# Fourteen products of the identity on TensorE while the first two chunks load

## The chip, the cores and the metric

One core of a Trainium2 chip. The metric is device microseconds (us) of one execution; lower is better. Executions of the same kernel spread by 2 to 3 us. The experiments ran in three batches, each on another chip, each with nine runs of the kernel before beside it; differences are taken within a batch unless the text says otherwise. The "granted clock" of a run is the mean share of full speed that the profile's records give TensorE.

## The reference

Retention over 64 (batch, head) sequences of 576 positions and 64 columns, followed by a maxout FFN:

```python
scores = (1 / sqrt(64)) * q @ k.T                    # per batch and head
ret = (scores * D) @ v                               # D[i, j] = gamma_h ** (i - j), 0 above the diagonal
x = ret, rearranged to (4608, 512)
h = maximum(maximum(x @ w1, x @ w2), x @ w3)         # (4608, 768), weights in float64
out = h @ w_out                                      # (4608, 512)
```

## The kernel before

The sequence is taken in 36 chunks of 128 positions. For each chunk K is scaled on GpSimd (POOL), K and Q are transposed on TensorE (PE), then come the scores, the state and the values. A group of four chunks feeds one pass of the FFN. The float64 weights arrive as integers, and VectorE (DVE), ScalarE (ACT) and POOL turn them into float32, piece by piece. The parts that matter here:

```python
def transposes(g):
    for n, src in (("k", kds[g]), ("q", raws.pop(("q", g)))):
        pt = ps_r.tile([P, NP, C], FP32, tag="r", name=n + "t")
        for p in range(NP):                              # NP = 4
            nc.tensor.transpose(pt[:, p, :], pair(src, p), ident[:C, :C])
        # ... copied to SBUF, K by DVE, Q by ACT

def scores(g):                                           # cut
    # 8 products s = K.T @ Q of 64 rows; DVE masks them: st
    for p in range(NP):
        nc.tensor.matmul(kv[:, p, :], lhsT=pair(kd, p)[r:], rhs=pair(raws["v", g], p)[r:], start=True, stop=True)
    # ... the state is made of kv on DVE and POOL

def down(t, h, m):                                       # cut
    for fb in range(NF):                                 # NF = 6: waits for each piece of w_out
        nc.tensor.matmul(ps[:], lhsT=h[:, fb, m * P:(m + 1) * P], rhs=w_sb["out", fb][:],
                         start=(fb == 0), stop=(fb == NF - 1))

# the beginning
load(0); load(1); load(2); load_weights(1); load(3); load_weights(2)
decay_keys(0); decay_keys(1)                             # POOL: kd
transposes(0)
transposes(1)
decay_keys(2)
scores(0)
transposes(2)
values(0)
decay_keys(3)
scores(1)
convert(4)                                               # first piece of the weights
transposes(3)
# ... cut
```

## Time and profile before

| | before |
|---|---|
| median of the first 3 runs | 888.28 us (887.31 to 889.44) |
| span of the profiled run, granted clock | 887.5 us, 0.996 |
| first transposes, first products at full speed | 5.21 us, 15.0 us |
| first weight conversion (expo) starts | 19.99 us |
| first `up` product starts | 35.21 us |
| first `down` product with the last piece of w_out | 121.10 us |

In the timeline a row has start, length, engine, line, operation, output<-inputs, shape and count, then the idle time before it and what ended it. In the chain of waits a row has start, length, and what held the end of the program at that time. In the table of windows below each row is a stretch of time: busy time and instructions of PE, its weight loads, DVE, ACT and POOL, then the granted clock, the DMA share and GB/s. Of the kernel before:

```profile
120.00:121.00 1.00, 0.00 (x0) 0.00 (x0) 0.00 (x0) 0.00 (x0) 1.00 (x1) 0.88 0.00 0
121.00:122.00 1.00, 0.90 (x1) 0.50 (x2) 0.00 (x0) 0.00 (x0) 1.00 (x2) 0.50 0.00 0
...
127.00:128.00 1.00, 1.00 (x3) 0.51 (x3) 0.69 (x1) 0.00 (x0) 0.00 (x0) 0.70 0.06 16
```

The clock column is at 0.50 from within the first row to within the last. In the first 15 us the same column shows 1.00.

### The profile page before, as it was taken

The page shows a single profiled execution, that of the slowest core. Times are in us where ns is not written, and L with a number is a line of the kernel's source. Part 1 is how long each engine was busy: PE and PEld are TensorE (multiplying, and loading weights), DVE is VectorE, ACT ScalarE, POOL GpSimd, SP SyncE. Part 2 cuts the span into 40 slices and gives each one's busy share as a digit, 9 for nine tenths or more (in the row PEclk, how much of TensorE's full clock was granted, in tenths as well). Part 3 has the DMA queues.
Part 4 walks back from the last instruction along what each step waited for, and adds up shares of the span by engine and source line. Part 5 has one row for each costly group of instructions (what it writes and reads, how often), then busy time and mean ns, then how long its engine had stood idle before and what let it go on. Part 6 is the DMA issues. An engine that isn't in the chain of part 4 may idle for free.

```text
span 887.5 us, 11310 instructions
## 1 busy us (share of the span) xinstructions
PE 870.8 (98%) x4544; PEld 639.5 (72%) x4544; DVE 371.4 (42%) x681; ACT 185.8 (21%) x391; POOL 141.4 (16%) x128
## 2 busy tenths in 40 slices
PE   6999989999999999999999999999999999999998
PEld 5645546887588858885788668875888578866883
DVE  3899944553244423443244324432433334422330
ACT  2455521111111102111111111111111111111211
POOL 3444424221110111001210011101111111001000
PEclk9999989999999999999999999999999999999999
DMA  9545614200150006000600033001600050000001
GB/s 235 154 138 173 179 49 121 57 1 12 57 123 1 1 36 154 1 1 24 147 21 1 13 96 83 1 1 49 142 1 1 24 130 1 0 25 24 1 1 47
DMA packets 128547, 51.58 MB, mean 58 GB/s; under 512 B 113648, under 2 KB 122864, under 8 KB 128496
## 3 DMA queue, kind: packets, MB, share of 16 engines
q1 hardware_dynamic: 128064, 50.34, 21.5%
q8 instruction: 36, 0.59, 0.3%
q10 hardware_dynamic: 432, 0.53, 0.2%
q14 instruction: 15, 0.12, 0.0%
HBM read 41.42 MB, written 9.44 MB: 57 GB/s over the span
## 4 chain that ended last, share of the span: by engine, by line
PE 87%; DVE 5%; ACT 3%; issue 2%; POOL 1%; DMA 1%; SPq 0%; DVEq 0%; POOLq 0%; ACTq 0%
PE x L292 28%; PE down L338 21%; PE z L292 14%; PE y L292 7%; PE s L155 4%; PE o L185 3%; PE kv L166 3%; PE o L190 3%; PE kt L141 2%; PE qt L141 2%; ACT expo L244 1%; ACT expo L248 1%; DVE expo L241 1%; DVE expo L252 1%; DVE h L352 1%
## 5 line engine op out<-in xcount | busy, mean ns | idle before, releaser
L338 PE MATMUL down<-wout,h 128*128 128x512 f32 x432 | 191.7, 597 | 3.8 <-POOL wout L255 3.8
L338 PEld LDWEIGHTS down<-wout,h 128*128 128x128 f32 x432 | 80.5, 191 | 96.5 <-issue 90.7
L292 PE MATMUL x<-S,T 128*128 128x256 f32 x576 | 147.8, 379 | 0.0
L292 PEld LDWEIGHTS x<-S,T 128*128 128x128 f32 x576 | 109.2, 190 | 15.1
L172 POOL TENSOR_TENSOR state<-state,gs 128x512 f32<-128x512 f32 x24 | 31.5, 1311 | 343.5 <-DVE state L171 296.5
L158 DVE TENSOR_TENSOR st<-s,causal 128x512 f32<-128x512 f32 x72 | 46.4, 686 | 76.5 <-PE s L155 76.5
L292 PE MATMUL x<-xT,w 128*128 128x256 f32 x288 | 74.9, 382 | 0.0
L292 PE MATMUL x<-S,w 128*128 128x256 f32 x288 | 74.3, 380 | 0.0
L292 PE MATMUL z<-xT,T 128*128 128x256 f32 x288 | 73.9, 379 | 0.0
L292 PE MATMUL z<-S,w 128*128 128x256 f32 x288 | 73.9, 379 | 0.0
L292 PE MATMUL y<-xT,w 128*128 128x256 f32 x288 | 73.9, 379 | 0.0
L297 ACT COPY p<-x 128x256 f32<-128x256 f32 x72 | 26.8, 372 | 182.8 <-PE x L292 182.8
L320 DVE TENSOR_TENSOR tmp<-x,p 128x256 f32<-128x256 f32 x48 | 20.4, 425 | 104.4 <-PE x L292 104.4
L347 PE MATMUL up<-xT,w 128*128 128x512 f32 x144 | 63.4, 593 | 0.0
L341 ACT COPY osb<-down 128x512 f32<-128x512 f32 x36 | 21.1, 586 | 202.1 <-PE down L338 202.1
L292 PEld LDWEIGHTS z<-S,w 128*128 128x128 f32 x288 | 54.7, 190 | 7.4
L292 PEld LDWEIGHTS y<-xT,w 128*128 128x128 f32 x288 | 54.7, 190 | 7.4
L292 PEld LDWEIGHTS z<-xT,T 128*128 128x128 f32 x288 | 54.1, 189 | 8.1
L292 PEld LDWEIGHTS x<-S,w 128*128 128x128 f32 x288 | 49.4, 189 | 13.2 <-issue 1.1
L192 DVE TENSOR_TENSOR xT<-o,gq 128x512 f32<-128x512 f32 x36 | 24.8, 690 | 72.8 <-PE o L190 66.8
L292 PEld LDWEIGHTS x<-xT,w 128*128 128x128 f32 x288 | 49.8, 191 | 5.5 <-issue 0.8
L130 POOL TENSOR_TENSOR kd<-kraw,gk 128x512 f32<-128x512 f32 x36 | 38.3, 1068 | 85.5 <-DMA kraw<-in_k_dram 74.9
(61 smaller groups left out, 913.9 us busy)
## 6 DMA issues: line engine op xcount, KB each, us to landing
bits<-in_moe_w_dram SPq DMA_DIRECT2D x18, 512.0 KB, 3.6
out_dram<-osb SPq DMA_DIRECT2D x36, 256.0 KB, 2.0
kraw<-in_k_dram SPq DMA_DIRECT2D x32, 256.0 KB, 4.0
qraw<-in_q_dram SPq DMA_DIRECT2D x32, 256.0 KB, 4.3
vraw<-in_v_dram SPq DMA_DIRECT2D x32, 256.0 KB, 4.3
bits<-in_moe_w_out_dram SPq DMA_DIRECT2D x6, 512.0 KB, 3.4
kraw<-in_k_dram SPq DMA_DIRECT2D x8, 128.0 KB, 3.6
qraw<-in_q_dram SPq DMA_DIRECT2D x8, 128.0 KB, 3.2
```

The source lines that it names most:

```text
L130: nc.gpsimd.tensor_tensor(t[:], raws.pop(("k", g))[:], gk[:].unsqueeze(2).to_broadcast([C, H, D]), op=ALU.mult)
L141: nc.tensor.transpose(pt[:, p, :], pair(src, p), ident[:C, :C])
L155: nc.tensor.matmul(s[j][:, p, :], lhsT=kT[r, p, :], rhs=qT[r, p, :], start=True, stop=True)
L158: nc.vector.tensor_tensor(st[:, j], s[j][:], masks[start_of(g)][:].unsqueeze(1).to_broadcast([C, NP, C]), op=ALU.mult)
L166: nc.tensor.matmul(kv[:, p, :], lhsT=pair(kd, p)[r:], rhs=pair(raws["v", g], p)[r:], start=True, stop=True)
L172: nc.gpsimd.tensor_tensor(t[:], t[:], gs[:], op=ALU.mult)
L185: nc.tensor.matmul(o[D * j:D * (j + 1), p, :], lhsT=vr[:, 2 * p + j, :], rhs=st[:, j, p, :], start=(p == 0), stop=(old == 0 and p == NP - ...
L190: nc.tensor.matmul(o[:, p, :old], lhsT=sd[:, p, :], rhs=qT[:, p, :old], start=False, stop=(p == NP - 1), skip_group_check=True)
L292: nc.tensor.matmul(out[:], lhsT=w[:, d * P:(d + 1) * P], rhs=xS[t][n][:, d, :], start=first and d == 0, stop=d == 1, skip_group_check=True)
L297: nc.scalar.copy(c[:], src[:])
L338: nc.tensor.matmul(ps[:], lhsT=h[:, fb, m * P:(m + 1) * P], rhs=w_sb["out", fb][:], start=(fb == 0), stop=(fb == NF - 1))
L347: nc.tensor.matmul(ps[:], lhsT=w_sb[i, fb][:, dc * P:(dc + 1) * P], rhs=xT[t][:, dc, :], start=(dc == 0), stop=(dc == NDC - 1))
```

## The change

The intent is that the array finds its full clock before the first real work needs it. TensorE multiplies the identity with itself while it would wait for the first loads; nobody reads the results.

```diff
+    def warm(n):
+        ps = ps_y.tile([P, P], FP32, tag="y", name="warm")
+        for _ in range(n):
+            nc.tensor.matmul(ps[:], lhsT=ident[:], rhs=ident[:], start=True, stop=True)
...
+    warm(9)
     load(0)
...
     transposes(0)
+    warm(5)
     transposes(1)
```

## The prediction

> **What bounds the kernel now.** I read the page first, slices and chain, then the chain of waits in order of time, the TensorE timeline of the first 24 us, the granted clock around 121 us and the landing of the first loads. From the page:
>
> ```profile
> span 887.5 us, 11310 instructions
> PE   6999989999999999999999999999999999999998
> PE 87%; DVE 5%; ACT 3%; issue 2%; POOL 1%; DMA 1%; SPq 0%; DVEq 0%; POOLq 0%; ACTq 0%
> ```
>
> The reader is to see that TensorE (PE) carries 87% of the path. It is idle only in the first slice (22.2 us each) and near 120 us. Whatever 14 more matmuls can bring lies in the first slice. The chain of waits, from its beginning, says which idle time counts (start us, length us, what):
>
> ```profile
> 3.05 5.06 DMA kraw<-in_k_dram
> 8.18 1.05 POOL kd L130
> 9.27 1.11 PE kt L141 x4
> 10.38 0.85 PE qt L141 x4
> 11.24 2.01 PE s L155 x16
> 13.25 1.92 PE kv L166 x8
> ...
> 16.05 1.02 PE o L185 x16
> 17.07 1.14 PE s L155 x16
> ...
> 20.08 0.35 DVE expo L241
> ...
> 119.78 1.27 POOL wout L255
> ...
> 121.10 2.07 PE down L338 x2
> ```
>
> So the load of the second K chunk and its scaling on POOL hold the path until 9.23 us; then TensorE holds it to 18.2; then the conversion of the float64 weights on DVE and ACT (rows expo, mant, frac) to 121.05; from there TensorE to the end. Conversion of one piece waits for the one before, so whatever moves its first step moves everything behind it. The timeline of TensorE shows what its 9 us are made of (start, length, operation):
>
> ```profile
> 5.21 1.12 PE L141 MATMUL kt<-ident,kd 128*128 128x128 f32 x4 [5.21 <-POOL kd L130]
> ...
> 11.17 2.08 PE L155 MATMUL s<-qT,kT 64*128 64x128 f32 x16
> 13.18 1.99 PE L166 MATMUL kv<-vraw,kd 128*128 128x128 f32 x8
> 15.01 0.60 PE L141 MATMUL kt<-ident,kd 128*128 128x128 f32 x4
> ...
> 17.00 1.16 PE L155 MATMUL s<-qT,kT 64*128 64x128 f32 x16
> 18.09 1.16 PE L166 MATMUL kv<-vraw,kd 128*128 128x128 f32 x8
> ```
>
> The same 16 score products take 2.08 us at 11.17 and 1.16 at 17.00; the same 8 kv products 1.99 and 1.16. The array ran at half speed until about 15.0 us, although the clock column of the page says 9 to 10 tenths there: no record covers this first stretch, only durations do. Half speed on the path is what the change aims at.
>
> **What the Trainium skill says.** (1) "TensorE: Matmul & The Clock Gate", Part 1: the array starts at half clock and goes to full after about one busy window of 3.4 us; the window is free-running. The trace agrees with halves, and with the period: in windows of one microsecond the granted clock is 0.88 in 120 to 121 and 0.70 in 127 to 128 with 0.50 between, so it fell at 120.76 and rose at 127.60, 6.84 us or two windows of 3.42. Stepped back 33 windows of the page's 3.413 us, 127.60 becomes 14.96, just where the durations halve. (2) The same page, "Why this matters for your kernels": keep TensorE busy 4 us or more, and leave no gap over about 3 us. (3) The same page, Part 4, says that transposes don't count as busy in the same way. The trace can't settle that, but the transposes do run faster once warm (1.12 us to 0.60 for four). No page says how busy a window must be.
>
> **The change part by part.** It removes and moves nothing. It adds 14 products of a 128x128 identity with itself, and two allocations from the two-buffer PSUM tag "y"; two keep the rotation where it was, nobody reads them, and the tag is not used again before the first `up` at 35 us. They need only the identity.
>
> Cost of one: the kv row is the same form (128 rows, 128 columns, fp32): in the chain 1.92 to 2.00 us for 8 cold, so 0.25 us; 1.09 for 8 warm, 0.14.
>
> Nine of them: the identity is finished on POOL at 1.38 (its last instruction starts at 1.09 and takes 0.29); plus about 0.1 of hand-over, start at 1.5. 9 x 0.25 = 2.25, end at 3.75. kd(0) lets the first transposes start at 5.21. So they delay nothing, and leave a gap of 1.46 us.
>
> Five of them: the first transposes end about 7.45; 5 x 0.25 = 1.25, end at 8.7. The next transposes start at 9.27. No delay, a gap of 0.57 us.
>
> So the direct cost on the path is nil and the benefit depends on when the clock rises. **If it is up by 9.27**, the path goes (warm durations from the later rows): kt and qt 0.88 to 10.15, s 1.09 to 11.24, kv 1.09 to 12.33. There it meets the third chunk: kd(2) is done at 12.72 (POOL from 11.68 for 1.04, released by a load), so transposes go 12.78 to 13.66, o 1.02 to 14.7, and s(1) starts at 14.7 in place of 17.0. Of a possible 2.85 us (half of 9.27 to 14.96), 0.45 is lost to that wait, leaving about 2.3. The masks and the state of chunk 1 then let the first expo start about 17.8 instead of 19.99; its weights landed at 16.5 (issued 10.62, 5.9 to landing), no obstacle. The fourth K chunk lands at 17.45 and kd(3) ends at 18.63 whatever TensorE does, so its transposes come only 0.3 earlier (18.98 to 18.7). With DVE taking its list in order I get s(2) ending and its mask ending at 24.1 against 25.6, the state of chunk 3 at 24.8 against 26.2, and the first `up` at 33.5 against 35.1: **about 1.6 us** that survive, and TensorE and the conversion both carry them on to 121 and so to the end.
>
> **How likely is it to be up?** On this trace's grid of windows (1.31, 4.72, 8.13, 11.55, 14.96):
> before, 8.13 to 11.55 was busy 9.27 to 11.55, 67%, and didn't raise it; 11.55 to 14.96, all busy, did. Near 121, the window 120.76 to 124.18 was busy from 121.10, at most 90%, and didn't raise it; the next, all busy, did. So a window must be nearly full. With the change: 1.31 to 4.72 is busy 2.25 of 3.41, 66%; 4.72 to 8.13 busy 5.21 to 8.13, 86%; 8.13 to 11.55 busy all but 0.57, 83%. By those precedents **none is enough**, and the clock would rise at 14.96 as before. At other phases the run 5.21 to 8.7, 3.5 us long, can hold a window, if transposes count.
>
> **Rivals.**
> A: the clock is up before 9.27, as intended. For it: the run of 3.5 us, an unknown threshold, and that nobody picks 9 and 5 without a reason. Against it: the two gaps. Gain 1.6 us against this profiled run; but its rise at 14.96 was late. If a window must start after 8.8 us, the rise before lies anywhere from 12.2 to 15.6; as 1.25 of the cold loss is absorbed, the mean gain over phases is about 1.1. Chance 0.4.
> B: the gaps undo it, and the time stays. For it: the precedents above and the page's Part 4. Chance 0.5.
> C: faster early TensorE is hidden anyway, since loads set the pace (POOL waited 12.0 us for K loads in the first 45 us). In part counted above: the loads of the third and fourth chunk eat 1.25 of 2.85. If the later conversion waits for a load at the earlier time too, A is worth 0.5. Chance 0.1.
> D: the added products are slower than kv, 0.43 each (four passes of 128 columns at the half clock would give that), and fill both gaps: nine end at 5.4, five at 9.6. That costs 0.2 to 0.3 and makes A sure. Against it: the kv rows. Included in A's chance.
>
> **Range and chances.** 0.4 x 1.1 + 0.1 x 0.5 = 0.5 us: 888.28 - 0.5 = 887.8; I put 887.7. The times of before spread over 887.31 to 889.44, and the phase of the clock's windows, at the start and again at 121 us, is reason enough for it. A full gain on a good median is 886; no gain on a poor one 889.2. Range 886.0 to 889.2. 2% is 17.8 us, over six times the whole cold loss of 2.85 us: same 0.97, faster 0.02, slower 0.01.
>
> **What would show it right or wrong.** In the timeline of the changed kernel: nine products from about 1.5, at a spacing of 0.25 us, and the end near 3.75 (D if near 5.3); five from 7.45 to 8.7; kt of chunk 0 still at 5.21 and of chunk 1 at 9.27. Then the score products at 11 us: 2.08 us long means B, 1.16 means A. With A: s(1) near 14.7, first expo near 17.8, first `up` near 33.5, first `down` pair after the conversion near 119.5 instead of 121.1. With C the first three move and the last does not. The prediction is wrong if transposes start late because of the added products, if `up` waits for the PSUM tag, or if the idle time near 118 us, falling on other windows, costs more or less than the cold stretch of 121.10 to 127.60 does now.

## The result, and the profile after

The changed kernel took 887.35 us (median of 6 runs, 886.27 to 888.40); the kernel before, with three more runs beside them, 888.56 (6 runs). The ratio is 0.9987, 95% interval 0.9974 to 1.0000: the same within 2%, as predicted, and close to the predicted 887.7. The interval reaches 1.0000, so this comparison alone doesn't show a gain. All outputs are right. A ratio is the mean time of one kernel's runs over the mean of the other's of the same rounds, so not quite the ratio of the medians.

From the page of the changed kernel, then its TensorE timeline:

```profile
span 884.6 us, 11367 instructions
```

```profile
1.43 4.21 PE L108 MATMUL warm<-ident 128*128 128x128 f32 x18 [1.43 <-POOL ident masks.py:199]
5.43 1.06 PE L147 MATMUL kt<-ident,kd 128*128 128x128 f32 x4
6.43 0.88 PE L147 MATMUL qt<-ident,qraw 128*128 128x128 f32 x4
7.15 1.28 PE L108 MATMUL warm<-ident 128*128 128x128 f32 x10
9.35 0.66 PE L147 MATMUL kt<-ident,kd 128*128 128x128 f32 x4 [0.91 <-POOL kd L136]
...
10.37 1.16 PE L161 MATMUL s<-qT,kT 64*128 64x128 f32 x16
...
15.02 1.16 PE L161 MATMUL s<-qT,kT 64*128 64x128 f32 x16
...
18.54 0.66 PE L147 MATMUL kt<-ident,kd 128*128 128x128 f32 x4 [1.27 <-POOL kd L136]
```

The reader should see three things. **First, x18 and x10:** each of the 9 and 5 products is two records, so nine fill the time from 1.43 to the first transposes (5.43 less 1.43 is 4.00, 0.44 us a product) where I had 2.25. There is no gap before 8.4 us. **Second,** the scores of chunk 0 take 1.16 us at 10.37 where they took 2.08 at 11.17: the clock was up. It rose at about 6.95, to judge by the fall and rise near 121 (119.58 and 123.00, and 34 windows of 3.413 us back from 123.00); the shorter row qt at 6.43 agrees, and the clock record in the trace file, which begins at the first rise, says 6.94. **Third,** the last row: TensorE now waits 1.27 us for kd(3). The chain of waits of the changed kernel says who brought it:

```profile
11.83 5.45 DMA kraw<-in_k_dram
...
17.44 1.05 POOL kd L136
18.49 0.04 issue
18.54 0.66 PE kt L147 x4
```

The load of the fourth K chunk has taken over the path that TensorE held from 9.27 to 18.2. What that leaves, in the two profiled runs:

| | before | after | earlier by |
|---|---|---|---|
| scores of chunk 1 start | 17.00 | 15.02 | 1.98 |
| first conversion (expo) starts | 19.99 | 18.01 | 1.98 |
| transposes of chunk 4 start | 34.28 | 32.80 | 1.48 |
| first `up` starts | 35.21 | 33.73 | 1.48 |
| `down` with the last piece starts | 121.10 | 119.59 | 1.51 |
| values (o) after the first `down` products start | 132.53 | 129.58 | 2.95 |
| span | 887.5 | 884.6 | 2.9 |

So 1.98 us was gained at the scores, 0.5 given back to the load, and 1.5 carried through the conversion to 121 us. The other 1.4 us appear after 121, where the change touched nothing. Here are the windows of the changed kernel there:

```profile
119.00:120.00 1.00, 0.41 (x1) 0.41 (x2) 0.00 (x0) 0.00 (x0) 1.00 (x2) 0.79 0.00 0
...
122.00:123.00 1.00, 1.00 (x12) 1.00 (x12) 0.00 (x0) 0.29 (x1) 0.00 (x0) 0.50 0.08 16
123.00:124.00 1.00, 1.00 (x14) 0.88 (x10) 0.56 (x1) 0.00 (x0) 0.00 (x0) 1.00 0.65 248
```

The half-clock stretch lasts 3.42 us here, one window, and 6.84, two windows, in the profile of before. Such a run has a granted clock of 0.998, the other kind 0.996. The profiled pair therefore flatters the change, and the experiments have to separate the two.

### The profile page after: what moved, and what is told of

Same layout as the page of the kernel before. It is cut to its first block, busy times and chain, and to the rows that moved or that the text cites. A ratio compares the mean times of both kernels' runs of the same rounds, so it can differ in the third digit from the quotient of the medians.

```text
span 884.6 us, 11367 instructions
## 1 busy us (share of the span) xinstructions
PE 871.5 (99%) x4572; PEld 640.8 (72%) x4572; DVE 371.4 (42%) x681; ACT 185.8 (21%) x391; POOL 141.5 (16%) x128
## 4 chain that ended last, share of the span: by engine, by line
PE 87%; DVE 5%; ACT 3%; issue 2%; SPq 1%; POOL 1%; DMA 1%; POOLq 0%; DVEq 0%; ACTq 0%
PE x L298 28%; PE down L344 21%; PE z L298 14%; PE y L298 7%; PE s L161 4%; PE o L191 3%; PE o L196 3%; PE kv L172 3%; PE kt L147 2%; PE qt L147 1%; ACT expo L250 1%; ACT expo L254 1%; DVE expo L247 1%; SPq L131 1%; DVE expo L258 1%
```

## The experiments

**Theory 1**: the products fill the windows, the clock rises before 9.3 us, and the path gains until the loads stop it. **Rival, luck**: the time moves only because the windows near 121 us fall otherwise. **Rival, place or number**: any product there helps, or only one of the two batches does. In each table "granted" lists the clocks of the 5 runs.

### The changed kernel twice more

> The changed kernel once more, on the chip of the other runs of this call. Theory 1 (the early clock): TensorE is busy from 1.43 to 7.4 us without a gap, a full window of 3.41 us always fits, the clock rises between 4.9 and 8.3 us, s of chunk 0 takes 1.16 us; 0.5 to 1.6 us less than before, and the same difference between runs of the same granted clock (0.996 with 0.996, 0.998 with 0.998). Rival (luck of the windows near 121 us): runs of the same granted clock differ by under 0.3 us from before.

> The changed kernel again, on the chip of these runs, for comparison. Theory 1: 0.7 to 2.0 us less than before; granted clock 0.996 to 0.998 in each run, never 0.994 or less (no fall in the first 20 us). Rival (luck): no difference from before when runs of 0.996 are compared with runs of 0.996.

| | mean, us | median, us | before, median | ratio (95%) | granted |
|---|---|---|---|---|---|
| after_again | 886.95 | 886.78 | 889.04 | 0.9978 (0.9965 to 0.9992) | 0.996 x2, 0.998 x3 |
| after_third | 886.40 | 885.71 | 888.65 | 0.9973 (0.9960 to 0.9985) | 0.996 x2, 0.998 x3 |

Both are faster than before. At equal granted clock, over all runs that have a clock on record (16 of the changed kernel, 32 of the kernel before, whose first six have none), chips mixed: at 0.996, 887.77 (8 runs) against 888.86 (26 runs); at 0.998, 886.07 (8) against 888.12 (6). Theory 1 asked for a difference within a class and finds 1.1 and 2.05; luck alone asked for under 0.3. The classes are not quite like with like, for the same clock can cost differently: of its 6.83 us at half clock near 121, the profiled run of after_third has a first window that is 52% busy, that of before one that is 90% busy. So the filled kernels below have to settle it. All in all, 886.92 against 888.72: 1.8 us, 0.2%. The gains of the means in the two batches, 1.9 and 2.3 us, are larger than expected (0.5 to 1.6, and 0.7 to 2.0).

The detail expected of after_again failed: its transposes of Q waited 0.60 us for a load, which left the window from 4.03 to 7.44 only 82% busy, and the clock was not up by 8.3 us but at about 10.85 (its fall at 120.08 less 32 windows). The second batch was cold, 2.34 us long, and the transposes of chunk 1 partly so (0.96 for kt, then 0.60 for qt). The scores still ran in 1.16 us.

### One batch alone

```diff
# first_only             # second_only            # small
     warm(9)             -    warm(9)             -    warm(9)
...                      ...                      +    warm(3)
-    warm(5)                  warm(5)             ...
                                                  -    warm(5)
                                                  +    warm(2)
```

> The nine products alone. Theory 1: the busy run 1.43 to about 7.4 us still holds a full window, and the gap of about 1.8 us to the transposes of chunk 1 empties none, so the clock rises by 8.3 us, s of chunk 0 takes 1.16 us and the gain is that of the changed kernel within 0.3 us. If the five products are needed to keep the clock, s of chunk 0 takes 2.08 us again in the profile and the gain is under 0.4 us.

> The five products alone. At the cold 0.44 us each they last from 7.4 to 9.6, delay the transposes of chunk 1 by about 0.3 us, and TensorE is busy from 5.21 on without a gap. Theory 1: the clock rises between 8.6 and 12.0 us, so part of s or kv of chunk 0 stays cold; 0.5 to 1.2 us less than before. Rival (luck near 121 us): no difference at equal granted clock.

> Three and two products in place of nine and five: the same instructions at the same places, but with gaps of about 2.4 and 1.0 us, so that no window before 9.3 us is full. Theory 1: clock rises at 12 to 15.6 us as before, s of chunk 0 takes about 2.08 us, time within 0.4 us of before. If added products as such help (without the clock), the gain stays near 1 us.

| | mean, us | median, us | ratio (95%), before 889.04 | granted |
|---|---|---|---|---|
| first_only | 888.88 | 888.54 | 0.9998 (0.9985 to 1.0010) | 0.994 x3, 0.992 x2 |
| second_only | 887.08 | 887.09 | 0.9978 (0.9965 to 0.9990) | 0.998 x2, 0.996 x3 |
| small | 888.33 | 888.84 | 0.9992 (0.9979 to 1.0004) | 0.996 x5 |

**first_only** is the most instructive miss. The timeline, and the windows, of its profiled run:

```profile
9.20 0.66 PE L147 MATMUL kt<-ident,kd 128*128 128x128 f32 x4 [1.85 <-POOL kd L136]
9.69 0.60 PE L147 MATMUL qt<-ident,qraw 128*128 128x128 f32 x4
10.22 2.42 PE L161 MATMUL s<-qT,kT 64*128 64x128 f32 x16
```

```profile
10.00:11.00 1.00, 1.00 (x9) 0.71 (x9) 0.58 (x1) 0.58 (x1) 0.07 (x1) 0.87 1.21 273
11.00:12.00 1.00, 1.00 (x12) 1.00 (x11) 0.00 (x0) 0.00 (x0) 0.97 (x1) 0.50 1.14 258
12.00:13.00 1.00, 1.00 (x7) 0.78 (x5) 0.66 (x2) 0.00 (x0) 0.00 (x0) 0.50 0.88 138
```

The clock rose early, for kt at 9.20 takes 0.66. But TensorE then idled for 1.85 us, and at 10.74 the clock fell again: the window from 7.33 to 10.74 was 46% busy. The scores took 2.42. All five runs have a granted clock of 0.994 or 0.992, one or two half-clock windows more than 0.996 holds, so the same very likely happened in each; only one was profiled. Nine products alone gain nothing here (the means differ by under 0.01 us). (Of the 2.42 us the half clock explains about 1.6. For the rest the trace shows that the first two and the last two of the 16 score records start one at a time, where in the changed kernel all start in pairs; why they do is open.)

**second_only** gained more than I expected (1.8 us of the means, interval 0.9 to 3.1). In its trace the K load of chunk 1 came late, kd(1) ended at 10.10 and the five products hid in that wait; scores took 1.37, so the clock rose during them, at about 12.6. That is later than the expected 8.6 to 12.0 and hardly earlier than the kernel before can have it (12.73 in fill_again below, which has no early products), so this trace doesn't explain the gain, and its cause stays open. Against the changed kernel on the same chip (886.95) it is not distinguishable: no run shows that the nine products add to what the five bring.

**small** is inconclusive in time, its interval holding zero as well as 1.9 us. Its trace shows a rise at 12.85 (the fall at 118.66 less 31 windows; 12.84 by the clock record; scores 1.71): no earlier than the kernel before can have it, as expected. That added products as such help is thus not excluded by its times.

### All in front

```diff
-    warm(9)
+    warm(14)
...
-    warm(5)
```

> All 14 products before the first transposes, none between. Theory 1 (what counts is a busy run without a long gap until 9.3 us, not the place): the transposes of chunk 0 come 1 to 2 us late, at 6.5 to 7.5, those of chunk 1 at most 0.4 late, the clock rises before 8.3 us and isn't lost in a gap as in first_only; s of chunk 0 takes 1.16 us, gain within 0.4 us of the changed kernel. If the place matters (transposes of chunk 0 are on the path), it is slower than the changed kernel by 1 us or more.

886.61 us against 888.65 before, ratio 0.9984 (0.9970 to 0.9998); mean 887.22. The first transposes came at 6.25, 0.8 us later than in the changed kernel, those of chunk 1 at 9.10: being late with chunk 0 cost nothing. But the gap of 1.82 us before chunk 1 is back, and one of five runs has the 0.994 of a fall. The profiled one kept its clock: its windows are 4.79 to 8.20 and 8.20 to 11.61, so the gap is shared by two of them, which stay 73% and 74% busy. In first_only a gap of the same size lay in one window. Its scores took 1.57, with the same single starts as in first_only. It is 0.8 us slower in the mean than the changed kernel in the same rounds (886.40), between the two limits set above, with a standard deviation of 1.3 in both, so I can't rank the two.

### The stretch near 121 us taken out

To size the early clock without that lottery, products of the identity also fill TensorE's waits for the last two pieces of w_out, in the kernel before (fill_only) and in the changed one (both):

```diff
+        fills = {NF - 2: 4, NF - 1: 10} if t == 0 and m == 0 else {}
         for fb in range(NF):
+            if fb in fills:
+                spare = ps_x.tile([P, P], FP32, tag="x", name="fill")
+                for _ in range(fills[fb]):
+                    nc.tensor.matmul(spare[:], lhsT=ident[:], rhs=ident[:], start=True, stop=True)
             nc.tensor.matmul(ps[:], lhsT=h[:, fb, m * P:(m + 1) * P], ...
```

> The kernel before, without the products at the start, but with four and ten products of the identity (into a spare PSUM tile) where TensorE waits for the last two pieces of w_out at 116 to 121 us. Theory 1: no window there is idle enough for the clock to fall, the granted clock is 1.000 for the whole span, the 3.42 or 6.84 us of half clock after 119 us are gone: 1.5 to 3 us less than before, and the runs spread less. If the products delay the last pieces instead, the gain is under 1 us and the first product of down with the last piece starts after 121.3.

> The changed kernel with the same products at 116 to 121 us. Theory 1: the early clock and the kept clock are independent and add: 0.5 to 1.5 us less than fill_only, 2.5 to 4.5 us less than before, around 885.5. Rival (the change only moves the windows near 121 us in luck): both and fill_only agree within 0.3 us.

> fill_only a second time, to size the early clock with the stretch near 121 us kept at full clock in both. If the rise of the clock lies anywhere from 12.2 to 15.6 us, the transposes of chunk 4 start between 33.5 and 34.9 (33.57 at a rise of 12.85, 34.28 at 14.96, 34.94 at 15.6 so far) and the time between 885.4 and 887.4. If the rise doesn't matter for the time, all runs lie within 0.4 us of 886.9.

> both a second time. The clock is up before 9.3 us at any phase, so the transposes of chunk 4 start at 32.4 to 33.0 and the time is 884.7 within 0.5; 1.1 (my recorded mean over the phases) to 2.2 us (as measured first) less than fill_again.

| | median, us | mean, us | before, median | ratio (95%) | granted |
|---|---|---|---|---|---|
| fill_only | 886.95 | 886.90 | 888.65 | 0.9978 (0.9966 to 0.9991) | 1.000 x5 |
| both | 884.65 | 884.74 | 888.65 | 0.9954 (0.9941 to 0.9966) | 1.000 x5 |
| fill_again | 885.44 | 885.78 | 888.59 | 0.9972 (0.9958 to 0.9985) | 1.000 x5 |
| both_again | 885.08 | 884.94 | 888.59 | 0.9961 (0.9948 to 0.9973) | 1.000 x5 |

The timeline of "both" near 121 us:

```profile
116.89 2.39 PE L348 MATMUL fill<-ident 128*128 128x128 f32 x20
119.79 1.13 PE L349 MATMUL down<-wout,h 128*128 128x512 f32 x2 [0.50 <-POOL wout L261]
120.84 1.16 PE L161 MATMUL s<-qT,kT 64*128 64x128 f32 x16
```

The `down` pair takes 1.13 us where it took 2.07, the scores 1.16 where 2.08, and the last piece arrives as before: its `down` starts 86.81 us after the transposes of chunk 4, and 86.82 in the kernel before, so the fill delays nothing (0.50 us of waiting is left). In fill_only this `down` started at 121.74, past the 121.3 that was to show a delay; but there too it is 86.80 us after chunk 4, which came late. The difference between filled kernels with and without the early products is 2.16 us in the first pair and 0.84 in the second; over 10 runs each 886.34 against 884.84, **1.5 us**, with an interval of about 0.7 either way worked out from their deviations of 0.86 and 0.53. The rival "luck" has no place to act here, since the clock is 1.000 in all 20 runs, and falls. Single pairs are noisier than I expected: 2.16 lies above 0.5 to 1.5, and 0.84 below 1.1 to 2.2.

The two pairs differ for the reason that fill_again was asked about: fill_only's trace shows kt of chunk 2 at 15.56 with 0.70, so the rise came late (15.76 by the clock record), and the transposes of chunk 4 at 34.94; fill_again's scores took 1.83 (rise at 12.73), and chunk 4 came at 33.33, a little under the expected 33.5. The later the rise, the later chunk 4, as expected. Conversely both_again started chunk 4 only at 33.75, outside my 32.4 to 33.0: its fourth Q chunk landed late and the transposes waited for it until 19.94. So in this trace a load, not the clock, set when chunk 4 starts.

### The kernel before against itself

> The kernel before against itself: ratio 1.000 within 0.001, which shows the floor of such comparisons; its trace gives another phase: clock rise at r between 12 and 15.7, the fall near 121 at r plus 31 or 32 windows of 3.413 us, and the transposes of chunk 4 at the start that belongs to r (33.5 at 12.8 to 34.9 at 15.6).

888.85 against 888.59, ratio 1.0004 (0.9992 to 1.0017). The transposes of chunk 4 started at 34.47. Its clock fell at 120.96 and rose at 124.38, one window; 31 windows before 120.96 is 15.15, where its transposes turn from cold to warm (kt of chunk 2 at 15.19 takes 0.60). The windows of the start and those of 121 us are one grid: in all 13 trace files the time from the first rise to the next fall is a whole number of windows of 3.413 us, to 0.01 us. These records also give each first rise directly: without early products at 14.96, 15.15, 15.76 and 12.73; with all 14, nine and five, at 6.94, 10.85, 4.94, 5.41 and 7.46, before 9.3 in four of five profiles.

How full must a window be? Some cases near the limits, with the window, and the share of it in which the profile has a TensorE product under way:

| kernel | window | busy | clock |
|---|---|---|---|
| before | 8.13 to 11.55 | 67% | stayed low |
| after_again | 4.03 to 7.44 | 82% | stayed low |
| before | 120.76 to 124.18 | 90.4% | stayed low |
| small | 9.43 to 12.84 | 90.5% | rose |
| before_again | 120.96 to 124.38 | 92% | rose |
| first_only | 7.33 to 10.74 | 46% | fell |
| second_only | 114.99 to 118.40 | 49% | stayed high |
| after | 6.95 to 10.37 | 73% | stayed high |

## Why the prediction was right or wrong

- **Right: the bound, and the course of rival A.** TensorE at half clock was on the path. The course of rival A came about: scores of chunk 1 near 14.7 (15.02), first expo near 17.8 (18.01), first `up` near 33.5 (33.73), `down` near 119.5 (119.59). The predicted 1.6 us against that profiled run measured 1.5, and the filled kernels, over ten runs each, gave 1.5 plus or minus 0.7 where I had 1.1.
- **In part luck: the number.** The predicted 887.7 was a mean over rivals in which B, held likeliest, is not what happened. It forecast a gain of 0.5 us; the first six runs gained 1.2, and all runs 1.8. The first runs of the changed kernel (mean 887.33) were also slower than its later ones (886.95 and 886.40), which brought the result nearer to 887.7.
- **Wrong: the cost of one product.** The step "the kv row is the same form ... so 0.25 us" divided the row by its 8 records. The loop has NP = 4 products; each float32 product is two records. A product costs 0.44 us cold (measured 4.00 for nine) and about 0.25 warm. I had the loop in front of me, and the Trainium skill's "FP8 and Floating Point Precision", TensorE Precision Notes, gives four passes for true float32: four times 128 columns at the cold clock of 1.2 GHz, which "TensorE: Matmul & The Clock Gate" gives in Part 1, are an estimated 0.43. The runs agree (records 0.213 us apart, two to a product).
- **Wrong in consequence: rival B at 0.5, the gaps of 1.46 us, and D set aside.** D is what happened. Its price was right too: the first transposes started 0.22 later (5.43 for 5.21) and nothing on the path felt it. Only its five did not end at 9.6: they ran warm and ended at 8.43, which left a gap of 0.91 us. With 0.44, the window from 1.31 to 4.72 of the prediction's own grid would have been 94% full, enough by its precedents, and A would have been the likeliest rival.
- **Right: a window must be nearly full.** The limit lies near 90% in these runs (90.4% stayed low, 90.5% rose). The argument from Part 4 of the clock page, that transposes might not count, fell: in the changed kernel the window that raised the clock, 3.53 to 6.95, holds 1.5 us of transposes, and would be 56% full without them, while 90.4% of products alone was not enough at 121 us.
- **Missed: that a raised clock must be held.** I weighed the gaps only for raising it. In first_only a gap of 1.85 us inside one window brought the clock down, and its five runs gained nothing; front14 shows that a gap of 1.82 us across two windows need not.
- **Rival C took its part:** the load of the fourth K chunk ate 0.5 of 1.98 us in the profiled pair, and it stands on the path now.
- **Half seen: the windows near 121.** I named them as a source of spread. What I did not see is that they move with the change: half of the changed kernel's runs (8 of 16) have the short stretch, and 6 of 32 before. If that is no accident it is worth some 0.4 us of the 1.8 (0.31 of the runs times 0.7 to 1.7 us between the classes). A reason offers itself, for in the kernel before the rise and the restart at 121 hang on the same grid, and in the changed one the restart doesn't depend on it; this is argued, not shown.

## What to carry to other kernels

Count records, not calls, when you price an operation from a row of the profile, and check the count against the loop. Warming the array took two things in these runs, one window full to about nine tenths and no later window under about half busy before the real work. Products in the gaps serve both, and here they cost nothing even where they delayed the first transposes by 0.2 us (0.8 more in front14). Whether both batches are needed is open: the five alone measured the same. Look for the same stretch in mid-kernel: filling the waits for the last weights gained 1.8 us here, about as much as the start, and doing both gave 884.65 us, 4 us less than the kernel before and, by the means, 1.7 less than the changed one in the same rounds.

## What the Trainium skill lacked or had wrong

- "TensorE: Matmul & The Clock Gate" says that the clock rises after a busy window and does not say how busy: 90.4% was too little and 90.5% enough here.
- The same page, "Why this matters for your kernels", allows idle gaps up to about 3 us. A gap of 1.85 us brought the clock down (first_only), because it left its window 46% busy; one of 1.82 us that was shared by two windows did not (front14, 73% and 74%), and 49% still held it once (second_only).
- The same page, Part 4, has transposes not raise the clock. Here a window with 1.5 us of float32 transposes in 3.41 raised it (after), and one with 1.9 us (fill_again, 9.32 to 12.73). No record says whether these calls use the mode that the page means.
- No page says that the clock records leave out the cold start: the column shows 1.00 during the first 15 us, when 16 score products took 2.08 us where 1.16 is full speed.
- No page that I read says that a float32 product appears as two matmul records: 9 products gave 18.
